# Two interleaved transformer layers on one core: riders' probabilities turned by a DMA, untiled TensorE groups run as column tiles, and a new order of the work

## The chip, the cores and the metric

The kernel runs on one core of a Trainium2 chip. A core has five engines that work side by side and wait for each other by semaphores: PE (TensorE; its weight loads are the row PEld), DVE (VectorE), ACT (ScalarE), POOL (GpSimd) and SP (SyncE, which issues the transfers here). The metric is the device time of one execution in microseconds, as the median of several runs; lower is better.

## The reference

Four sub-layers follow one another over 2048 tokens of width 448, each added to its input: attention with a recurrent memory (A), a gated MLP (B), A again, B again, with the same weights both times.

```python
def A(x, mem0, Wq, Wk, Wv, Wo):        # 64 segments of 32 tokens, 16 heads of 256
    mem = mem0                          # 8 rows
    for s in range(64):
        h = concat([mem, x[32*s:32*s+32]])             # 40 rows
        q, k, v = h @ Wq, h @ Wk, h @ Wv               # per head
        p = softmax(mask(q @ k.T / 16))                # 40 x 40; a token sees the memory rows and earlier tokens
        o = sum over heads of (p @ v) @ Wo
        mem, out[s] = o[:8], o[8:]
def B(x): return (relu(x @ W_gate) * (x @ W_up)) @ W_down      # 448 -> 1792 -> 448
x = x + A(layernorm(x)); x = x + B(layernorm(x)); x = x + A(layernorm(x)); x = x + B(layernorm(x))
```

## The kernel before

**Folding.** At the start `weights` forms one product of Wq and Wk for every head (tile `A`, SBUF) and one of Wv and Wo (`Bsb`). For that each weight half of 256 columns is turned on PE against an identity (`transposes`, L709, eight 128-column turns), copied to SBUF, and multiplied (`product`, L722). The raw Wq and Wk come by DMA into eight staging slots `Wst`; a head pair `g` takes four slots, and each slot is one load of 512 columns in two transfers (`load`, L684). The first product needs the turned first halves of all four slots. A warm-up group `spin` (L627) of 11 matmuls on zeros stands at the head of the program's list.

**The chain.** Segment s needs the memory that segment s-1 leaves. `chain(step)` runs steps 0 to 70: the memory rows of layer 0 at segment `step` and of layer 1 at segment `step - 7` go together. One step is: memory times `A` (L891, 64x32 tiles), copy and turn on DVE (L1065, L1073), scores (`middle`, L1088), softmax on DVE and ACT, turn P on PE (L1121) and copy it (`PT`), P times h (L1145, L1148), times `Bsb` (L932, 128x32 column tiles, 56 matmuls), split into two bf16 parts (`Ohi`, `Olo`), back into rows of the next memory (`cols`, L951, eight matmuls of 32 columns). The new rows `Rsb` go to the tiles `HR` by a copy for layer 0 and by small DMAs for layer 1.

**Riders.** L891 and L932 have room for 32 rows, and the memory uses 16. From step 7 on the other rows carry token rows of layer 1's even tiles, the "riders" (66 passes of `middle` with a mask, of lower rank than the chain; their y is needed by the next step's L932). Their rows leave by small DMAs `Tsb<-Rsb`.

**Tiles.** The token rows proper are worked per 128 tokens: `att_group` (L1234 in 64x128 tiles, scores L1260, softmax, turn of P L1279, y L1145, output L1309 untiled in three groups of 5, 5 and 4 matmuls of 448 columns), the MLP (`glu_units` L1333 in 64x128 tiles, `glu_down` L1352 untiled), and `norm` with a turn on PE (L1180).

**Order.** `_Sched` lists every operation with engines, a cost in ns, what it reads and writes, and a `mode`: 0 untiled, 1 column tiles of 128x32, 2 row tiles of 64x128, 3 column halves, 4 tiles of 64x32. The order of PE is written out by hand: each character of the string `LINE` says which of the groups still left comes next (a `~` skips 80). The other engines' orders come out of the planner `schedule`, by earliest start, rank and `ORDER`, with fixed costs: 94 ns (`TURN`) where PE's mode changes, 2400 ns (`LAND`) from a transfer to its landing. A gap that it foresees on PE is filled with dummy matmuls (`filler`, L1367). Every engine then runs its list strictly in order. DMAs take semaphores in turn out of `N_DMA` = 48; at the end SP waits for the last 48 (L392 to L395).

Of the kernel before, what the change touches and what calls it, by code (L numbers as in the profile page):

```python
# [32 lines left out]
ORDER = ("apBEFEsrpdlvwtalsfVTmkVGVHZcgovZUZYfyHHZvnNZAeQbcMbewfTnUFUQvUgaoeqBAiOnO0I0rv0lMkrKnz0r0uAaQNEaNQQazYeabwswaa"  # L33
         "kachNaueDaDnraBi0VaaaEgchNAXKfqPTdYLCyXA0vXuAOMMuO0NTaaajla0sKIRXEYQtW000wNsLjwIkZxNdPhpEaFWfCWPsaP0azdGgppTTs"
         "bfxQ0LhUZmVLLYpzOWWVheCpFacuzUaZoawVWvTdGTClViASRXlmhReM0pS0nuALXNRpGATz0RgjtdlAlInioyUoUnX0EJmWLBaQraHHgEouJy"
         "bgxcnwtPWaEwhaPDlTbAvF0FJZnHqUttyQIg0otagAaIklTzbYuw0squomrJAAAsAxgfYHR0c0f0YCdJKysxYHj0zmAgzyluvSEk0aKpSp0AIl"
         "SAhJiaASaAjxutpkdukQvXH0pf0d0OUdICCoteize0GWGJgbDCAYcYyuaUPaFwGEN0ufHAAosgdnlSiXvsBKRpLSPeJ0U0AdQQNoVdiAxBtbcm"
         "hQfFe0gK0z0El0XzAABafzaoEaRbnwtcelFvOzxSIHsgGuHAIXeDJAP0AXYdLdduBBRaXAXlTaR0a0BUMhhWLAelHAaP0DgayjFfYkBiBuWidV"
         "WiEYJkPoVscRkU0GPwDmebCeAxOwj0KcwGOspsFauwazTgIY0HfAEv0KtqKAaSmMagVKYxtbPQOj0vhW0wZWXdckUYaxYatAjeUTDVfArZgA0J"
         "ZxLSOaznuQoCnfqdyEgiNX0bmeNghhUWctiX0XITkAZNUhGAcyoSAUWPa0AakgETBEqGbfApnOAwd0yYs0eQWssMwOfAn0lAmfLvjLZA0WHaMq"  # L40
         "abHJwwdZxSpjVJqGdIaXVYVftvYDmJPTLpTmjnssZgsANROGVOcAKzpflogjfAdoanAANOKUraGtaGmvpaa0iLDhoZulYn0fTqA0TAG00EKzbs"
         "wtVAqHgyXueoaSNaspOSrpZ0RHCRikLlDqA0KoMwXoONJmAPmqdyWy0ijMNrHoTONMl0YhHFxhyjwdAtY0o0gTyWaDQdadZNmT0zs0gVmtaaaa"
         "aag0fNKUTaaaaaaaaaaaaaaaaaaaqjtECNTsaxWawbsV")

SIGNS = "ABCDEFGHIJKLMNOPQRSTUVWXYZabcdefghijklmnopqrstuvwxyz0123456789+-*/=<>()[]{}.,:;!"
LINE = ("IGGFNNMLGGFHFFOFMBJIHHFFEFEMMLFHFEEFEMEBLAAEEFDDBBBBIIDDDDCCBBBIIFBBBDBBABAIHEEBACBAJBLAOHLFBDCCAAgAeeAdBFBCLA"
        "XoBAEUCTBBSBQBKOCBMECBABHUAGGBAAbBAQBJAQAWAFBADPAECCCADIMFIIALEOOEFLEGAEDGFACAABAAWAAAKARBAPHdAcGASAQAAABT~EA~"
        "DAihKA(DAdAAbAa9AZZZAAXBAAADTSDDAAAAMAAKKKJAIIAHAHGABBDAABBAAAAAATMYYAAWKcKKZAM~JNAVkLA~MAAAEEAHDAaZFFCCGCASBB"
        "QABOSAAMMMAAKALLuA0KICIHHLHHHAGGGGGAAADJAABBAEAAAABAMAAXXQAGIaASHHWAGAAAFQDBDDAFBEEYXAAFAASAAQCBOARNNNAALANM4A"
        "uLJQCJIIBHHHAFGFnHGFcAADAABBAEAAABCAAMBAXXQAJcKJZSALeAdLKAAAQEEIATDA87GneF3CC7A0BEyAfDDuuuAAsAEtsFEoAACmCAkSoh"  # L50
        "hhKggg9BAeIVfeABAAaYEAAAVATTLAAQQQDAAONGOAONBfAVcLUACHAHMGGaBFFFBUAGDRKDxxF~PETAtGACqAAoNDClllmAAJQDAgfACB=ccc"
        "ADACCAWAbAUATAWSSSA0zDQARQAAOAAALAJJCIIIALIHAUIIgAeAGAAaEABQKBBaJIiBBBUFHBEBPAD}{DtsCA>BB=[CA*OCB999ALAC55mD44"
        "Ck1AAzADAwABWycsjBBpppApf=nDFnmlDDPDhDAlfCCdDcccCebAabbaBGBFIAUAAAAWQIDOUDNNNAPAAvDIIAH87CNCV3AAA05CzIyyyCHxAA"
        "uuBKssAQQwpJDAAlC(BjAJhhhDAAeC/BeeADAZDCAXAAAUAYTStSSSASgBCAAAMAAYABBbVIAAneTGGQZgAFXAAbPDAB5B3MLBBBFFJFBADA>>"
        "FRQE[*mABB8B7ACA8HBB111AEAyAAxxmdvAAbiqqvIpFFFmmmFdlFjFFjiAA/GD+leAAHbiaaBHYYYCJCWVAqVVUAC0dARAAAOBS0NCBAKKKNK"
        "JDKI54DVHDAAyADAv0DuMCsssABDpAHnoo.CMCAADiAnCffGCdAcccEAAaZACBXXAAAATpwTYAtRAQAPPPBAAMAAZAAkAJHaUfVHHHjAAPFAQA"
        "kUMDAABLeBBBaHBEB}{NHACC>CQCA*GA+jAA777AA65BA65AbAi1zADYAwAvuktttAtAaADoFppDDnDDTiNDDgGfLydDcccFcAacAcbBFBWXAG"
        "AaATASRXEDPPPAANPAM=/DAJA9<ZIA6A5NM3334AkLAYAPxDvAvuCTCAEAoAOAlGpCj.Biii-EAgAfCCeeAEAAAgZ2CBXAWVAAASSSASgABAAN"
        "AAAYACAjVIZBATSHGZgGARAADjASCBWLLcBBBLFPFBEAA)(FQFCHC-CC9AJB-A5nB333BkcFziAzzFYEAvA0AUsqhqp{pppBBAmmRAllRACOAA"
        "fAAjAcAbaAZZZAbYJXGYXIBUAGSAAAPUAOFNNNFNAVVvLEASI87hDID+3AAF0ADyYxxxAxAvAAuuALAJqACHtNAlBj>jBADgggEDAAcEAcc8ED"  # L60
        "AAWeXAAAUZASSkSSSAnSBABAAALAAWAiAHTYAAcRFFhPfFAAcPMDARAJJBIaILBBBJtUIFBEBPHDDA88ppEECC28lHCABxBAv~KvvvXDtAAUss"
        "ADEpAumEmlCk<kkkCaNhABhhEKDcAcIRZZAAcXBWWWFNBUTGBSSSFAEgOVOAAAAKDQOEITDLHHHIAAFKAAABxwBLBKbrEBBuHnAmNBkkkLBjiA"
        "DIggE.DdAAEaAAYAX*CBVVVAVATAAUTRAoQQDBOBNAMMMdALLAZAADCAHTYAnGGQQZZEFRdSRFAZSED3DDDHHDGDI]]ItISLFDA*AC+Ak8AA+6"
        "667AA4CG43BFAAzAAxB1vveuuudAAurrjutqAFADoxuEDkl+DkjGiiiDiMDDgeeDEfeDbbDDZKeDDWdDNU9DTTTATARKADZZOvQDdWAMATLBRL"
        "QQQEQAANJNPPDGCJAKAAGACFAEDXDDDATCABBPWIHAAZAQAWJOAIICQDDAAGDDAEDABEAIEDAAAAAADBAAADAAAACAAAAAA")


class _Op:
    __slots__ = ("idx", "engs", "cost", "fn", "deps", "prio", "dma", "eng", "ndep", "users", "ready",
                 "start", "end", "need_inc", "val", "clock", "slot", "seq", "alloc", "mode",  # L70
                 "touch", "busy", "cross", "at")
# [16 lines left out]
class _Sched:  # L88
# [5 lines left out]
    N_DMA = 48  # L94
# [28 lines left out]
    def add(self, engs, cost, fn, r=(), w=(), prio=None, dma=0, alloc=(), room=(), mode=0, now=None, busy=None, cross=False, at=0):  # L123
# [7 lines left out]
        o.at = at  # L131
        o.deps = {}
# [62 lines left out]

    def schedule(self):
# [35 lines left out]
        while left:  # L232
# [55 lines left out]
            if o.dma:  # L288
                free[e] = t0 + c
                dma_free = max(dma_free, t0) + o.dma / 240.0  # L290
                o.end = dma_free + self.LAND
# [32 lines left out]
    def filler(self, n, ns, bank, deps, start, seq):  # L324

        f = _Op()
        f.at = 0
        f.idx, f.engs, f.cost, f.eng, f.dma, f.touch, f.mode = -1, ("pe",), {"pe": n * ns}, "pe", 0, [], 0
# [11 lines left out]
    def emit(self, nc, stack, block):  # L340
# [41 lines left out]
        def run(eng, E):  # L382
            if eng == "act":
                E.preload_act_table_set("natural_log_exp_and_others")
            for o, waits, inc in plans[eng]:
                for key, v in waits:
                    E.wait_ge(dsem[key[1]] if isinstance(key, tuple) else sems[key], v)
                ins = o.fn(E, eng)
# [30 lines left out]
def copy_any(out, in_, scale=None):  # L419
# [8 lines left out]
    return fn  # L428

# [54 lines left out]
class _Kernel:  # L484
# [39 lines left out]
    def alloc(self):  # L524
# [32 lines left out]
        for p in range(NPAIR):  # L557
            for k in range(4):
                for hh in range(2):
                    c = D * (b_idx(k, p, hh) if k < 3 else b_tail(p))  # L560
                    self.s.alias[("B", p, hh, k)] = [(w, i) for w in ("Wst", "Wst3", "Wst4") for i in range(12) if c < 2048 * i + 2048 and 2048 * i < c + D]
# [45 lines left out]
    def constants(self):  # L607
# [17 lines left out]
        def spin(E, e):  # L625
            for _ in range(11):
                i = E.matmul(wb.ap()[:, 0:D], lhsT=hG[:, 0:128], rhs=hG[:, 128:576], start=True, stop=True)  # L627
            return i
        s.add("pe", 11 * 378, spin, r=hk, w=[wb], alloc=[wb])
# [45 lines left out]
    def dma(self, dst, src, nbytes, r=(), w=(), prio=None):  # L675
        return self.s.add("sp", 750 if nbytes < 8192 else 640, lambda E, e: E.dma_start(dst, src), r=r, w=w, dma=nbytes, prio=prio)

    def turned(self, dst, src, nbytes, r, w, prio=None):

        self.s.add("sp", 900, lambda E, e: E.dma_start(dst, src, transpose=True), r=r, w=w, dma=4 * nbytes, prio=prio)  # L680

    def weights(self):
        s = self.s
        def load(src, p, slot):  # L684
            s.part()
            c0 = 512 * p
            self.dma(self.Wst[slot][:, 0:3, :], src[64:448, c0:c0 + 512].rearrange("(k p) c -> p k c", p=128), 393216,
                     w=[("Wst", slot)])
            if slot < 8:
                self.dma(self.Wst[slot][0:64, 3, :], src[0:64, c0:c0 + 512], 65536, w=[("Wst3", slot)])  # L690
            else:
                self.dma(self.Wst[slot][0:64, 3, 0:256], src[0:64, c0:c0 + 256], 32768, w=[("Wst3", slot)])
                self.dma(self.Wst[slot][64:128, 3, 256:512], src[0:64, c0 + 256:c0 + 512], 32768, w=[("Wst4", slot)])

        def transposes(slot, hh, wt, rot):
# [4 lines left out]
            keys = [("Wst", slot), ("Wst3", slot), ("Wz", slot, 0)] + ([("Wst4", slot), ("Wz", slot, 1)] if slot >= 8 else [])  # L700
# [161 lines left out]
    def chain(self, step):  # L862
# [84 lines left out]
        def cols(E, e):  # L947
            for k in range(4):
                for q, O in enumerate((hi_, lo_)):
                    w = O[:, 128 * ((k + 1) % 4):128 * ((k + 1) % 4) + 128]  # L950
                    x = E.matmul(br.ap()[:, 32 * k:32 * k + 32], lhsT=w, rhs=self.Sel[:, :], start=(q == 0), stop=(q == 1))  # L951
            return x
        s.add("pe", mm_cost(*[32] * 8), cols, r=["Ohi", "Oli", "Oh2", "Ol2", "Sel"], w=[br], alloc=[br], room=MEM + ["mC"], **P)
# [26 lines left out]
        for slot, q, o in out:  # L980
            for v in range(4):
                to, of = self.row_piece(self.Tsb[32 * q + 8 * o:32 * q + 8 * o + 8, :], R[32 * v + 8 * slot:32 * v + 8 * slot + 8, :], v)
                self.dma(to, of, 2048, r=[rk], w=[("Tsb", q, o, v)])
# [91 lines left out]
    def middle(self, act, m, row, col, P):  # L1075
# [32 lines left out]
        else:  # L1108
# [7 lines left out]
            for c, sg, l in act:  # L1116
# [3 lines left out]
        bp = self.bank("C", "G")  # L1120
        s.add("pe", 56, lambda E, e: E.matmul(bp.ap().bitcast(BF)[:, 0:128], lhsT=m["P"][:, :], rhs=self.ident[:, :], is_transpose=True),  # L1121
              r=[k_("P"), k_("P0"), k_("P1"), "ident"], w=[bp], alloc=[bp], **P)
        s.add(EV, ev_cost(128, fast=True), copy_any(m["PT"][0:104, :], lambda: bp.ap().bitcast(BF)[0:104, 0:128]), r=[bp], w=[k_("PT")], **P)
# [33 lines left out]
    def norm(self, t, dst):  # L1157
# [20 lines left out]
        def tr(E, e):  # L1178
            for k, o in enumerate(BLOCK):
                x = E.matmul(pk()[:, k, :], lhsT=xn[:, o:o + 128], rhs=self.ident[:, :], is_transpose=True)  # L1180
# [311 lines left out]
```

## Time and profile before

| | |
|---|---|
| time, median of 3 runs | 1509.2 us (1508.84 to 1509.79) |
| the profiled execution | 1510.83 us, of which the span from first to last instruction is 1509.0 us |
| PE busy | 1486.1 us (98%), 36999 matmuls |
| DVE, ACT, POOL busy | 77%, 59%, 8% |
| bytes moved by DMA | 34 MB, nearly all in the first 65 us |
| share of PE in the chain that ended last | 95% |

A line of a group gives line, engine, operation, output<-inputs, shapes, count, then busy time in us and mean ns of one, then the engine's idle time before them and what ended it. Matmuls are pipelined, so one of 448 columns shows as 353 ns while the next starts 189 ns later; what counts for PE's time is the distance from start to start. A timeline line gives start in us, length in us, and what ran.

### The profile page before, as it was taken

What the parts mean: (1) busy time and instruction counts of PE and PEld (TensorE: products, weight loads), DVE (VectorE), ACT (ScalarE), POOL (GpSimd) and SP (SyncE); (2) the same over time, 40 slices, a digit from 0 to 9 for tenths busy, and PEclk for the clock granted to TensorE, in tenths of its full rate; (3) what the DMA queues carried; (4) which work ended last, traced back from release to release, by engine and by line L of the source; (5) the groups of instructions that cost most, each with busy time, mean ns of one, the idle gap of its engine ahead of it and who ended that gap; (6) DMA issues with size and microseconds to landing.
All of it is one profiled execution on the core that took longest, in us unless ns stands there. A gap on an engine that the chain in (4) does not pass through costs nothing.

```text
span 1509.0 us, 82702 instructions
## 1 busy us (share of the span) xinstructions
PE 1486.1 (98%) x36999; PEld 1059.0 (70%) x36999; DVE 1167.8 (77%) x3574; ACT 891.9 (59%) x2407; POOL 120.1 (8%) x483
## 2 busy tenths in 40 slices
PE   7999999999999999999999999999999999999999
PEld 5657666666767777777767677777768777677776
DVE  6767788788888888687877788788877788688764
ACT  8775465566555656565655556566555556555543
POOL 1000000010000010000000010010100000010000
PEclk9999999999999999999999999999999999999999
DMA  8512100000000000000000000000000000000000
GB/s 244 169 30 74 40 8 12 11 9 8 8 5 12 11 8 15 4 18 4 18 5 8 14 9 14 4 18 6 17 6 8 14 8 15 5 8 8 11 6 14
DMA packets 60658, 34.08 MB, mean 23 GB/s; under 512 B 31744, under 2 KB 60176, under 8 KB 60304
## 3 DMA queue, kind: packets, MB, share of 16 engines
q1 hardware_dynamic: 60304, 28.80, 7.4%
q8 instruction: 291, 4.77, 1.3%
q14 instruction: 63, 0.52, 0.1%
HBM read 21.36 MB, written 1.84 MB: 15 GB/s over the span
## 4 chain that ended last, share of the span: by engine, by line
PE 95%; DVE 2%; ACT 1%; DMA 1%; issue 1%; SPq 0%; POOL 0%; DVEq 0%
PE psG L1234 17%; PE psG L1309 17%; PE psG L1333 11%; PE psC L932 10%; PE psC L891 8%; PE psG L1352 5%; PE psG L891 4%; PE psG L1145 3%; PE psG L722 3%; PE psG L1260 3%; PE psC L1088 2%; PE psC L1145 2%; PE psG L709 1%; PE psG L932 1%; PE psG L1180 1%; PE psC L951 1%
## 5 line engine op out<-in xcount | busy, mean ns | idle before, releaser
L1234 PE MATMUL psG<-HT,A 64*128 64x128 bf16 x4924 | 287.2, 216 | 1.0 <-issue 0.6
L1309 PE MATMUL psG<-Bsb,YT 128*128 128x448 bf16 x1344 | 286.2, 353 | 0.0
L1234 PE MATMUL psG<-HX,A 64*128 64x128 bf16 x3693 | 267.6, 216 | 0.0
L1234 PEld LDWEIGHTS psG<-HT,A 64*128 64x128 bf16 x4924 | 235.7, 94 | 14.0 <-issue 8.3
L424 ACT ACTIVATE Ug<-psG 64x128 bf16<-64x128 f32 (+2 forms) x456 | 160.7, 372 | 63.7 <-PE psG L1234 54.7
L1234 PEld LDWEIGHTS psG<-HX,A 64*128 64x128 bf16 x3693 | 195.2, 94 | 0.1
L1309 PEld LDWEIGHTS psG<-Bsb,YT 128*128 128x128 bf16 x1344 | 118.1, 97 | 97.9 <-issue 7.8
L1333 PE MATMUL psG<-G,glu 64*128 64x128 bf16 x5880 | 185.6, 216 | 0.7 <-issue 0.4
L1333 PEld LDWEIGHTS psG<-G,glu 64*128 64x128 bf16 x5880 | 171.8, 94 | 11.2 <-issue 8.4
L932 PE MATMUL psC<-Bsb,YTm 128*32 128x448 bf16 x3304 | 167.3, 353 | 0.3
L1065 DVE STREAM_TRANSPOSE uT<-Usb 128x384 bf16<-128x384 bf16 x280 | 154.6, 559 | 6.1 <-ACT Usb L424 1.8
L891 PE MATMUL psG<-A,mT 64*32 64x448 bf16 x4004 | 144.8, 350 | 0.5 <-issue 0.5
L891 PE MATMUL psC<-A,mT 64*32 64x448 bf16 x3836 | 140.8, 350 | 0.1
L424 ACT ACTIVATE YT<-psG 128x448 bf16<-128x448 f32 x254 | 128.3, 544 | 10.3 <-PE psG L1148 8.9
L932 PEld LDWEIGHTS psC<-Bsb,YTm 128*32 128x32 bf16 x3304 | 82.8, 97 | 65.1 <-ACT YTm L424 1.6
L427 DVE CAST Ug<-psG 64x128 bf16<-64x128 f32 (+2 forms) x250 | 104.8, 430 | 16.0 <-PE psG L1234 11.8
L940 ACT ACTIVATE Ohi<-psC 128x448 bf16<-128x448 f32 x122 | 46.9, 384 | 116.4 <-PE psC L932 85.5
L1338 ACT ACTIVATE hG<-psG 128x512 bf16<-128x512 f32 (+1 forms) x125 | 67.7, 543 | 72.3 <-PE psG L1333 65.6
L891 PEld LDWEIGHTS psC<-A,mT 64*32 64x32 bf16 x3836 | 71.9, 92 | 50.0 <-DVE mT L427 3.9
L941 DVE TENSOR_TENSOR Olo<-psC,Ohi 128x448 bf16<-128x448 f32 x122 | 51.4, 422 | 71.5 <-ACT Ohi L940 70.8
L1339 DVE TENSOR_TENSOR hG<-hG,psG 128x512 bf16<-128x512 bf16 (+1 forms) x116 | 70.7, 614 | 29.5 <-ACT hG L1338 28.0
L1352 PE MATMUL psG<-glu,hG 128*128 128x448 bf16 x420 | 92.4, 352 | 0.0
(223 smaller groups left out, 2874.4 us busy)
## 6 DMA issues: line engine op xcount, KB each, us to landing
HR<-xn SPq DMA_DIRECT2D x128, 32.0 KB
Tsb<-Rsb SPq DMA_DIRECT2D x256, 1.5 KB
Tsb<-Rsb SPq DMA_DIRECT2D x256, 2.0 KB
Bsb<-in_A_Wq_dram SPq DMA_DIRECT2D x8, 384.0 KB
Bsb<-in_A_Wk_dram SPq DMA_DIRECT2D x8, 384.0 KB
HR<-Rsb SPq DMA_DIRECT2D x126, 1.5 KB
HR<-Rsb SPq DMA_DIRECT2D x126, 2.0 KB
X<-in_A_x_dram SPq DMA_DIRECT2D x16, 112.0 KB
```

The costliest lines, as they stand in the source:

```text
L424: return E.activation(out, i, ACT.Copy, scale=1.0 if scale is None else scale)
L427: return E.tensor_copy(out, i)
L891: i = E.matmul(ub[v].ap()[32 * j:32 * j + 32, 0:D], lhsT=self.mT[rw, WHERE[b], first:first + 32], rhs=cols, start=(b == 0), stop=(b == 6), ...
L932: x = E.matmul(bo.ap()[32 * j:32 * j + 32, 0:D], lhsT=self.YTm[:, q, :], rhs=self.Bsb[:, chunks[q], :], start=(i == 0), stop=(i == 13), ti ...
L1065: self.s.add("dve", 578, lambda E, e, out=out, hh=hh: E.transpose(out, heads[hh]), r=[("Usb", 2 * half + v) for v in range(2)], w=[f"uT{ha ...
L1145: return E.matmul(ps[:, n * q:n * q + n], lhsT=HR[rows, 128 * q:128 * q + 128], rhs=PT, start=True, stop=True, tile_position=(b, 0))
L1234: i = E.matmul(ub[v].ap()[:, 128 * n:128 * n + 128], lhsT=self.A[rw, b, a0:a0 + 128], rhs=HT[rw, WHOLE[b], :, 0:SEG] if CROSS[b] is None e ...
L1309: i = E.matmul(bo.ap()[:, 0:D], lhsT=YT[:, c, :], rhs=self.Bsb[:, 14 * g + c, :], start=(g == 0 and c == 0), stop=(g == 3 and c == 13))
L1333: i_ = E.matmul(two[v].ap()[:, 128 * c:128 * c + 128], lhsT=self.Wgu[rw, b, f0:f0 + 128], rhs=G[rw, WHOLE[b] if CROSS[b] is None else 4 + ...
L1338: s.add("act", 170 + 0.833 * N, lambda E, e, dst=dst, z=two[0], N=N: E.activation(dst, z.ap()[:, 0:N], ACT.Relu), r=[two[0]], w=[("hG", i, ...
L1339: s.add("dve", dv_cost(N), lambda E, e, z=two[1], N=N, dst=dst: E.tensor_tensor(dst, dst, z.ap()[:, 0:N], ALU.mult), r=[two[1]], w=[("hG", ...
L1352: i_ = E.matmul(bk.ap()[:, 0:D], lhsT=hG[:, c, :], rhs=self.Wd[:, c, :], start=(c == 0), stop=(c == NFC - 1))
```

## The change

- **Riders' P.** In `middle`, where there is a mask, the turn on PE and the copy from PSUM are left out; `turned` issues a transposing DMA on SP from P to PT. Planned cost: 1400 ns on SP, 3500 ns to land.
- **Column tiles.** A group may name a second mode: `also=(1,)`. `line` goes through the order, keeps runs of groups whose modes agree, and gives each run one mode, the lowest possible. So an untiled group becomes mode 1 only where it stands in a run with a group that is mode 1 alone (L932, and the two first steps' L999 and L1022). In mode 1 `packed` issues four matmuls of 32 output rows in place of one of 128. The groups that may do so: L1309, L1352, L1279, L1180, L951, and L1121 (the chain's).
- **First weights in halves.** The four loads of the first head pair are split into columns 0 to 255 and 256 to 511, first halves first, with the highest rank. The warm-up has 17 matmuls.
- **The plan.** 96 semaphores for DMAs in place of 48; 3500 ns to land for `HR<-xn`, `Tsb<-Rsb` and the turned P; new strings `ORDER` and `LINE`. (The name of the change speaks of blocks of 256 instructions: no line of the diff has them; they can only have gone into the strings.)

```diff
-    N_DMA = 48
+    N_DMA = 96
...
-        return out + left
+        out += left
+        run, have = [], None
+        for o in out + [None]:
+            may = {o.mode, *o.also} if o else set()
+            if have is not None and not have & may:
+                for x in run:
+                    x.mode = min(have)
+                run, have = [], None
+            have = may if have is None else have & may
+            run.append(o)
+        return out
...
+def packed(E, mode, out, lhsT, rhs, **k):
+
+    if mode != 1:
+        return E.matmul(out, lhsT=lhsT, rhs=rhs, **k)
+    for j in range(4):
+        q = slice(32 * j, 32 * j + 32)
+        i = E.matmul(out[q], lhsT=lhsT[:, q], rhs=rhs, tile_position=(0, 32 * j), **k)
+    return i
...
-            for _ in range(11):
+            for _ in range(17):
...
-        self.s.add("sp", 900, lambda E, e: E.dma_start(dst, src, transpose=True), r=r, w=w, dma=4 * nbytes, prio=prio)
+        self.s.add("sp", 1400, lambda E, e: E.dma_start(dst, src, transpose=True), r=r, w=w, dma=4 * nbytes, prio=prio, land=3500.0)
...
-                    load(W, g + 4 * v, slot[v, i])
+                    load(W, g + 4 * v, slot[v, i], (0, 1) if g else (0,))
+            if not g:
+                for v in range(2):
+                    for i, W in enumerate((self.Wq_d, self.Wk_d)):
+                        load(W, g + 4 * v, slot[v, i], (1,))
...
-                    x = E.matmul(br.ap()[:, 32 * k:32 * k + 32], lhsT=w, rhs=self.Sel[:, :], start=(q == 0), stop=(q == 1))
+                    x = packed(E, e, br.ap()[:, 32 * k:32 * k + 32], w, self.Sel[:, :], start=(q == 0), stop=(q == 1))
...
+        if m["mask"] is not None:
+            self.turned(m["PT"][:, :], m["P"][:, :], 32768, [k_("P"), k_("P0"), k_("P1")], [k_("PT")], prio=P["prio"])
+            bp = None
+        else:
+            bp = self.bank("C", "G")
...
-                    i = E.matmul(bo.ap()[:, 0:D], lhsT=YT[:, c, :], rhs=self.Bsb[:, 14 * g + c, :], start=(g == 0 and c == 0), stop=(g == 3 and c == 13))
+                    i = packed(E, e, bo.ap()[:, 0:D], YT[:, c, :], self.Bsb[:, 14 * g + c, :], start=(g == 0 and c == 0), stop=(g == 3 and c == 13))
```

More of the change, by code (lines that the diff above doesn't have):

```diff
@@ L121, in part, with add @@
         self.shift = 0.25 * (STEPS.index(ORDER[self.unit]) - 26) if self.unit < len(ORDER) else 0.0
-    def add(self, engs, cost, fn, r=(), w=(), prio=None, dma=0, alloc=(), room=(), mode=0, now=None, busy=None, cross=False, at=0):
+    def add(self, engs, cost, fn, r=(), w=(), prio=None, dma=0, alloc=(), room=(), mode=0, now=None, busy=None, cross=False, at=0, also=(), land=None):
         o = _Op()
@@ L131, in add @@
         o.at = at
+        o.also = also
+        o.land = land or self.LAND
         o.deps = {}
@@ L290, in schedule @@
                 dma_free = max(dma_free, t0) + o.dma / 240.0
-                o.end = dma_free + self.LAND
+                o.end = dma_free + o.land
             elif e == "pe":
@@ L678, in turned, with load @@
     def turned(self, dst, src, nbytes, r, w, prio=None):
-        self.s.add("sp", 900, lambda E, e: E.dma_start(dst, src, transpose=True), r=r, w=w, dma=4 * nbytes, prio=prio)
+        self.s.add("sp", 1400, lambda E, e: E.dma_start(dst, src, transpose=True), r=r, w=w, dma=4 * nbytes, prio=prio, land=3500.0)
     def weights(self):
         s = self.s
-        def load(src, p, slot):
-            s.part()
+        def load(src, p, slot, halves=(0, 1)):
+            if halves != (1,):
+                s.part()
@@ L686, in load @@
             c0 = 512 * p
+            if slot < 8:
+                a, b = 256 * halves[0], 256 * halves[-1] + 256
+                n = b - a
+                self.dma(self.Wst[slot][:, 0:3, a:b], src[64:448, c0 + a:c0 + b].rearrange("(k p) c -> p k c", p=128), 768 * n,
+                         w=[("Wst", slot, h) for h in halves], prio=0 if len(halves) == 1 else None)
+                self.dma(self.Wst[slot][0:64, 3, a:b], src[0:64, c0 + a:c0 + b], 128 * n, w=[("Wst3", slot, h) for h in halves],
+                         prio=0 if len(halves) == 1 else None)
+                return
@@ L982, in chain @@
                 to, of = self.row_piece(self.Tsb[32 * q + 8 * o:32 * q + 8 * o + 8, :], R[32 * v + 8 * slot:32 * v + 8 * slot + 8, :], v)
-                self.dma(to, of, 2048, r=[rk], w=[("Tsb", q, o, v)])
+                self.dma(to, of, 2048, r=[rk], w=[("Tsb", q, o, v)], land=3500.0)
         for f in late:
@@ L1119, in middle @@
                       r=[k_("Em"), k_("rc")], w=[k_(f"P{c}")], **P)
[L1120 to L1123, printed above, removed]
+        if m["mask"] is not None:
[3 more added lines that the diff above has]
+            bp = self.bank("C", "G")
+        if bp: s.add("pe", 56, lambda E, e: packed(E, e, bp.ap().bitcast(BF)[:, 0:128], m["P"][:, :], self.ident[:, :], is_transpose=True),
+              r=[k_("P"), k_("P0"), k_("P1"), "ident"], w=[bp], alloc=[bp], also=(1,), **P)
+        if bp: s.add(EV, ev_cost(128, fast=True), copy_any(m["PT"][0:104, :], lambda: bp.ap().bitcast(BF)[0:104, 0:128]), r=[bp], w=[k_("PT")], **P)
         yb = [self.bank("C", "G") for _ in act]
@@ L1179, in tr @@
             for k, o in enumerate(BLOCK):
-                x = E.matmul(pk()[:, k, :], lhsT=xn[:, o:o + 128], rhs=self.ident[:, :], is_transpose=True)
+                x = packed(E, e, pk()[:, k, :], xn[:, o:o + 128], self.ident[:, :], is_transpose=True)
             return x
@@ L1187, in norm @@
             G = self.G2[g]
-            s.add("pe", mm_cost(*[128] * 4), tr, r=xnk + ["ident"], w=[bk], alloc=[bk], room=[("G2", g, v) for v in range(3)])
+            s.add("pe", mm_cost(*[128] * 4), tr, also=(1,), r=xnk + ["ident"], w=[bk], alloc=[bk], room=[("G2", g, v) for v in range(3)])
             s.add(EV, ev_cost(512, fast=True), copy_any(G[:, 0:4, :], pk), r=[bk], w=[("G2", g, 0)])
@@ L1195, in norm @@
         HT, HX = self.HT[l][b], self.HX[l][b]
-        s.add("pe", mm_cost(*[128] * 4), tr, r=xnk + ["ident"], w=[bk], alloc=[bk], room=[("HTx", l, b), ("HX", l, b, 0), ("HX", l, b, 1)])
+        s.add("pe", mm_cost(*[128] * 4), tr, also=(1,), r=xnk + ["ident"], w=[bk], alloc=[bk], room=[("HTx", l, b), ("HX", l, b, 0), ("HX", l, b, 1)])
         for p in range(2):
@@ L1278, in pt @@
             for p in range(2):
-                i = E.matmul(bp.ap().bitcast(BF)[:, 128 * p:128 * p + 128], lhsT=Pf[:, 128 * p:128 * p + 128], rhs=self.ident[:, :],
-                             is_transpose=True)
+                i = packed(E, e, bp.ap().bitcast(BF)[:, 128 * p:128 * p + 128], Pf[:, 128 * p:128 * p + 128], self.ident[:, :], is_transpose=True)
             return i
-        s.add("pe", mm_cost(128, 128), pt, r=[("Px", si), "ident"], w=[bp], alloc=[bp], room=["PTx"])
+        s.add("pe", mm_cost(128, 128), pt, r=[("Px", si), "ident"], w=[bp], alloc=[bp], room=["PTx"], also=(1,))
         s.add(EV, ev_cost(256, fast=True), copy_any(PT[0:104, :], lambda: bp.ap().bitcast(BF)[0:104, 0:256]), r=[bp], w=["PTx"])
@@ L1351, in fn @@
                 for c in range(4 * q, 4 * q + n):
-                    i_ = E.matmul(bk.ap()[:, 0:D], lhsT=hG[:, c, :], rhs=self.Wd[:, c, :], start=(c == 0), stop=(c == NFC - 1))
+                    i_ = packed(E, e, bk.ap()[:, 0:D], hG[:, c, :], self.Wd[:, c, :], start=(c == 0), stop=(c == NFC - 1))
                 return i_
-            s.add("pe", mm_cost(*[D] * n), fn, r=[("hG", i, q), f"Wd_{q}"], w=[bk], alloc=[bk] if q == 0 else ())
+            s.add("pe", mm_cost(*[D] * n), fn, r=[("hG", i, q), f"Wd_{q}"], w=[bk], alloc=[bk] if q == 0 else (), also=(1,))
         self.add_x(t, bk)
```

91 lines of the change are left out of this document (45 added, 46 removed).

## The prediction, made before the changed kernel ran

> **What bounds the kernel now.** I read first the shares of the chain that ended last and the slices of the page, then the groups by line, then PE's timeline.
>
> ```profile
> PE   7999999999999999999999999999999999999999
> ...
> PE 95%; DVE 2%; ACT 1%; DMA 1%; issue 1%; SPq 0%; POOL 0%; DVEq 0%
> ...
> L1309 PE MATMUL psG<-Bsb,YT 128*128 128x448 bf16 x1344 | 286.2, 353 | 0.0
> L932 PE MATMUL psC<-Bsb,YTm 128*32 128x448 bf16 x3304 | 167.3, 353 | 0.3
> ```
>
> PE is the bound from 8.6 us on, so only what PE's own sequence loses or gains counts; ACT and DVE work that disappears is worth nothing. I therefore split the span by PE's records, start to start: nothing until 8.6 us; 1417 us in which groups stream (among them 5.4 us of filler matmuls and 6.5 us of pauses inside groups); some 615 changes of tile shape; 17.4 us of pauses over 20 ns at 81 group borders beyond the cost of a change; 3 us of tail. Walking `LINE` over the list of groups gives 614 changes of mode, so string and trace agree. The price of one change is seen here:
>
> ```profile
> 708.28 0.93 PE L1352 MATMUL psG<-glu,hG 128*128 128x448 bf16 x4
> ...
> 709.45 0.22 PE L1121 MATMUL psC<-ident,Pr 128*128 128x128 bf16 x1
> 709.51 0.92 PE L1352 MATMUL psG<-glu,hG 128*128 128x448 bf16 x4
> ...
> 710.26 0.18 PE L951 MATMUL psC<-Sel,Ohi 128*128 128x32 bf16 x1
> 710.29 0.18 PE L951 MATMUL psC<-Sel,Olo 128*128 128x32 bf16 x1
> ...
> 714.18 0.35 PE L891 MATMUL psG<-A,mT 64*32 64x448 bf16 x1
> 714.47 0.34 PE L1145 MATMUL psG<-PTx,HR 40*128 40x128 bf16 x6
> ```
>
> From the last start of L891 (714.18) to L1145 (714.47) are 290 ns; 448 columns stream in 190, so the change costs about 95. Over all records the median is 92 to 98 ns for every pair of shapes. One rider's turn is 54 to 60 ns of PE (709.45 to 709.51). L951 places matmuls of 32 columns 25 ns apart.
>
> **1. Changes of mode.** Walking the new `LINE` with the rule of `line` gives 579 changes, 35 fewer: 35 x 95 = **-3.3 us**. Without the second mode the same order would have 660. The runs turn 80 groups of L1309, 16 of L1352, 26 of L1279, 20 of L1180 and 24 of L951 into column tiles; the chain's L1121 never.
>
> **2. The riders' turns.** 66 x 54 ns = **-3.6 us**. Leaving them out alone changes no count of modes (36 of 66 stand between untiled groups).
>
> **3. The price of column tiles.** For 448 columns there is a row: 56 matmuls of L932 take 2667 ns, 14 of L1309 take 2640, so 27 ns in 14, some 9 ns for a group of 5: 96 x 8 = +0.7 us. For 128 and 32 moving columns in four tiles no row exists. Lower end: the tiles run side by side, and a group only pays some 12 ns of stagger (the four starts of L932 lie 3 to 4 ns apart): 70 x 12 = +0.9. Upper end: each small load and matmul takes the 25 ns of L951, one after another: L1279 8 x 25 = 200 in place of 109, L1180 16 x 25 = 400 for 221, L951 32 x 25 = 800 for 192; 26 x 91 + 20 x 179 + 24 x 608 = +20.5 us. Nearest is L891: eight loads and matmuls start within 27 ns and repeat every 191 ns, 23.9 ns each, set by the 448 columns and not by loads; and L1148 (two row tiles of 64 columns) starts one every 14 ns. Both speak for side by side: **+1.6 us**.
>
> The Trainium skill (TensorEngine Tiling, Restrictions and Gotchas) says that column tiling excludes the fast weight load; its page TensorE: Matmul & The Clock Gate (LDWEIGHTS) prices a load at columns / 1.2 ns, so an estimate of 27 ns for 32 columns, as much as a full fast one. If four such loads queue, that is the upper end above; L999, four tiles of 256 columns, repeats every 0.11 us, which neither shows nor excludes it.
>
> **4. The head.**
>
> ```profile
> 8.57 1.89 PE L709 MATMUL psG<-ident,Bsb 128*128 128x128 bf16 x16 [8.57 <-DMA Bsb<-in_A_Wk_dram]
> ...
> 11.32 3.29 PE L709 MATMUL psG<-ident,Bsb 128*128 128x128 bf16 x40
> 14.54 2.84 PE L722 MATMUL psG<-glu 128*64 128x448 bf16 x28
> ...
> 21.87 2.41 PE L709 MATMUL psG<-ident,Bsb 128*128 128x128 bf16 x40
> ...
> 28.36 2.24 PE L627 MATMUL psC<-hG 128*128 128x448 bf16 x11
> ...
> 30.55 2.84 PE L722 MATMUL psG<-glu 128*64 128x448 bf16 x28
> ```
>
> The first 16 turns stand 110 ns apart, those at 21.87 about 56: PE starts at half speed and speeds up near 13 us. The first product comes at 14.54, after seven groups of turns. Now the 17 warm-up matmuls run from about 1.3 us while PE would idle, so the turns run at 56 ns. A transfer takes 0.58 us of SP; its first packet comes 1.1 us after its issue, its semaphore 1.3 us after the last. The new order turns the four first halves, then the second halves of slots 0 and 2, before the first product. Slot 2's second half is the 13th and 14th transfer, issued to 8.9 us, landed near 11.4 us; 0.45 us for its turns: first product at 11.9, with six groups done instead of seven: 14.54 - 11.9 - 0.45 = **-2.2 us** (0 if packets of 512 bytes or the copies behind the turns hold it up; -4.5 if the data comes as early as it is wanted). SP's later loads are moved back by 8 more issues, 4.6 us; the first product of the second pair is wanted after 18 us, when they have landed. The 11 warm-up matmuls at 28.36 disappear: the products behind them have their inputs by about 29 us, so 30.55 - 28.95 = **-1.6 us** (0 to -2.1).
>
> **5. Fetches of instructions.** Counting PE's instructions, some 14 pauses with no wait fall on position 193 to 195 of a block of 256, in all 4.0 us. The diff has nothing for them but the order itself; the column tiles add some 4400 instructions to 74000. **-2 us** (-4 to +1).
>
> **6. Other stalls and fillers.** 17.4 + 6.5 + 5.4 us of pauses and fillers, less the fetches and the filler in the head (1.0), leave some 24 us. Here the planner's belief matters: it gave a transfer 2.4 us to land.
>
> ```profile
> 846.26 3.45 DMA HR<-xn
> ...
> 850.45 3.68 DMA Tsb<-Rsb
> ...
> 855.97 0.37 PE psC L951 x8
> ```
>
> DVE waits in order for `Tsb`, the chain's `Olo` behind it is late, and PE stands 1.15 us before L951. The new 3.5 us is right for these. Only a few stalls have such a cause; most lie at 100 to 350 us, where the chain has too little other work. The new order's distances in the chain (L951 to L891, L1088 to L1121) are equal or a little longer. **-3 us** (-10 to +5).
>
> **7. The turned P as a wait.** P to PT took 0.53 us on PE and ACT; now SP needs 1.4 us by the plan, and PE waits in order at the rider's L1145, with the whole kernel behind it. The score's start to P took 3.5 us in the median. Between a rider's scores and its y the new order puts at least 6.9 us of PE work; 4 riders have under 8, 12 under 9, 17 under 10. A transposing DMA has no row. Lower end: 3.45 us, as `HR<-xn` of the same 32 KB; upper: 16384 single elements at 8 ns (the smallest packets) on 16 engines add 8.2, so 11.6 us. I take 4.5 as it is nearest to the row of equal size: ready 8 us after the scores, and the shortfall below 8 us sums to 3.2, of which the quickest P save a part: **+2 us**. On SP 66 x 1.4 = 92 us join 697; behind one stand only transfers for the next step, some ten us away.
>
> The Trainium skill (Advanced Engine Details and Errata, X-Bar Transpose) holds transposing transfers to be as fast as plain ones; by it this term would be about 0; no run here shows it yet.
>
> **8. The tail.** After the last store SP waits for 48 semaphores in pairs, 61 ns each, from 1507.08 to 1508.56; the store had landed by then. 48 more are 24 x 61 = **+1.5 us**.
>
> **Sum.** -3.3 - 3.6 + 1.6 - 2.2 - 1.6 - 2 - 3 + 2 + 1.5 = -10.6. The profiled execution took 1510.83, so 1500.2; the median lies 1.6 below that execution: **1498.6 us**.
>
> **Rivals.**
> - *The stalls stay* (0.16): the new order is no better in places 4 (first term), 5 and 6, and only what is counted remains: -10.6 + 7.2 = -3.4, 1505.8. For it: the order before came from the same planner and still left 24 us.
> - *The column tiles' loads queue* (0.08): term 3 becomes 0.7 + 20.5, so +9.0, 1518.2, slower. It decides from half of the upper end on. Against it: L891 and L1148.
> - *The turned P lands late* (0.13): slower. Place: L1145 of the riders; if PT is ready 10 us after the scores instead of 8, the shortfalls of 17 riders sum to 23.8 us: -10.6 - 2 + 23.8 = +11.2, 1520.4. At 9.2 us it eats the whole gain; at 15 us it would be 150 us.
> - *The forecast* (0.63).
>
> Faster or slower by under 0.2% (3 us) is about what a measurement cannot tell from no change. Faster: 0.63, most of the first rival, and mild forms of the others, 0.76; same 0.08; slower 0.16. The range takes the good ends of 4 to 6 (some -10) and reaches to mild forms of the two slower rivals: 1488 to 1514.
>
> **What would show it.** Changes of tile shape near 579; L709 at 56 ns from the first; first L722 near 12 us; no L627 later; no PE wait for a DMA at L1145 of PTr; a packed L951 group of some 0.2 us (0.8 if loads queue), from its first start to the next group; SP's last waits 3 us long. I am wrong if PE waits for PTr in dozens of places, or if fillers and pauses add up to more than the 29 us of before.

## The result, and the profile after

The changed kernel takes **1514.69 us** (median of 6 runs, 1512.50 to 1516.30) where the kernel before takes 1509.61 beside it: ratio **1.0033 (95%: 1.0020 to 1.0046)**, some 5 us slower. 1498.6 was predicted, in a range up to 1514. The profiled execution has a span of 1513.3 us, 4.3 more than before.

From the page of the changed kernel: PE's slices, the shares of the chain that ended last, and the group that was L932 before.

```profile
PE   8999999999999999999999999999999999999998
...
PE 94%; DVE 3%; ACT 2%; issue 1%; POOL 0%; DVEq 0%; POOLq 0%
...
L966 PE MATMUL psC<-Bsb,YTm 128*32 128x448 bf16 x3472 | 178.1, 353 | 0.9 <-DVE YTm L440 0.8
```

PE is still the bound, and its first slice is fuller (the warm-up runs from 1.2 us), but DVE and ACT have won two points of the chain: PE stands behind them more often. To see where, I set the traces side by side at the same finished work of PE (every group at one standard price; riders' turns, fillers and warm-up matmuls count as none). Microseconds behind the kernel before, when that kernel stood at the time on top:

| | 13.6 | 27.4 | 35.2 | 45.3 | 61.6 | 100.6 | 875.9 | 1493 |
|---|---|---|---|---|---|---|---|---|
| changed | -0.2 | +0.8 | -1.2 | +0.3 | **+4.1** | +4.2 | +1.9 | +3.6 |

After 62 us the changed kernel gains little and gives it back; single executions of the same instructions drift 1 to 2 us apart there, so the last two columns say no more than that. The loss sits between 35 and 62 us. First the stretch where it was to win, PE of the changed kernel:

```profile
1.22 6.13 PE L651 MATMUL psC<-hG 128*128 128x448 bf16 x17 [1.22 <-DVE hG L646]
7.29 1.96 PE L739 MATMUL psG<-ident,Bsb 128*128 128x128 bf16 x32
11.95 0.62 PE L739 MATMUL psG<-ident,Bsb 128*128 128x128 bf16 x8 [2.71 <-ACT glu L437]
12.41 1.17 PE L1404 MATMUL psC<-ident 128*128 128x128 bf16 x18
13.41 0.61 PE L739 MATMUL psG<-ident,Bsb 128*128 128x128 bf16 x8
13.95 2.84 PE L752 MATMUL psG<-glu 128*64 128x448 bf16 x28
```

The turns are warm (32 in 1.96 us), yet the first product starts at 13.95, not 11.9: PE waits 2.71 us for an ACT copy. ACT in the same stretch:

```profile
7.61 3.49 ACT L437 ACTIVATE glu<-hG 64x256 bf16<-64x256 bf16 x8
11.00 2.52 ACT L437 ACTIVATE glu<-psG 128x896 bf16<-128x896 bf16 x3
```

Until 11.0 us ACT copies zeros (`glu<-hG`, fills of the staging slots); only then come the turned weights (`glu<-psG`) that were in PSUM from 9.25 us on. Now the stretch of the loss, PE of the changed kernel and of the kernel before:

```profile
47.99 1.07 PE L739 MATMUL psG<-ident,Bsb 128*128 128x128 bf16 x16
48.89 0.61 PE L1404 MATMUL psC<-ident 128*128 128x128 bf16 x8
49.77 0.55 PE L752 MATMUL psG<-glu 128*128 128x448 bf16 x2 [0.27 <-DVE glu L440]
50.16 1.06 PE L739 MATMUL psG<-ident,Bsb 128*128 128x128 bf16 x16
...
56.24 0.55 PE L1404 MATMUL psG<-A 128*128 128x448 bf16 x2
57.03 1.52 PE L925 MATMUL psC<-A,mT 64*32 64x448 bf16 x56 [0.24 <-DVE A L439]
```

```profile
47.33 2.41 PE L709 MATMUL psG<-ident,Bsb 128*128 128x128 bf16 x40
49.58 3.69 PE L722 MATMUL psG<-glu 128*128 128x448 bf16 x32
```

Before, forty turns (five groups) are followed by 32 product matmuls without a gap: the copies of the first turns end while PE turns the last. After, two groups of turns are followed at once by the product that needs their copies; fillers (L1404) and waits stand where the copies run. In the stretch that holds this loss (34.0 to 65.7 us of the changed kernel) fillers take 3.6 us and waits 1.8, where the same work of the kernel before has no filler and under 0.2 us of waits. Some 2 us stand at the three places of this kind (43.8, 48.9 and 51.4 us), 0.8 at 56.2, where the first product with `A` stands right behind the copy into `A`, 0.5 at 61.4 is a late fetch of instructions (last section), and most of the rest waits for ACT's copies of earlier products.

### The profile page after: what moved, and what is told of

Same layout as the page of the kernel before. It is cut to its first block, busy times and chain, and to the rows that moved or that the text cites. A ratio compares the mean times of both kernels' runs of the same rounds, so it can differ in the third digit from the quotient of the medians.

```text
span 1513.3 us, 87244 instructions
## 1 busy us (share of the span) xinstructions
PE 1489.1 (98%) x39223; PEld 1066.7 (70%) x39223; DVE 1166.3 (77%) x3552; ACT 884.8 (58%) x2365; POOL 117.6 (8%) x481
## 4 chain that ended last, share of the span: by engine, by line
PE 94%; DVE 3%; ACT 2%; issue 1%; POOL 0%; DVEq 0%; POOLq 0%
PE psG L1272 17%; PE psG L447 17%; PE psG L1370 11%; PE psC L966 11%; PE psC L925 9%; PE psG L450 5%; PE psG L925 4%; PE psC L447 3%; PE psG L1183 3%; PE psG L752 3%; PE psG L1298 3%; PE psC L1183 2%; PE psC L1122 1%; PE psG L966 1%; PE psG L739 1%; PE psG L1186 1%
## 5 line engine op out<-in xcount | busy, mean ns | idle before, releaser
L447 PE MATMUL psG<-Bsb,YT 128*128 128x448 bf16 x875 | 186.7, 352 | 0.0
L966 PE MATMUL psC<-Bsb,YTm 128*32 128x448 bf16 x3472 | 178.1, 353 | 0.9 <-DVE YTm L440 0.8
L925 PE MATMUL psG<-A,mT 64*32 64x448 bf16 x4116 | 159.7, 350 | 1.0 <-issue 1.0
L925 PE MATMUL psC<-A,mT 64*32 64x448 bf16 x3724 | 150.6, 350 | 1.2 <-DVE mT L440 0.4
L437 ACT ACTIVATE YT<-psG 128x448 bf16<-128x448 f32 x245 | 124.0, 544 | 20.2 <-PE psG L1186 19.4
L966 PEld LDWEIGHTS psC<-Bsb,YTm 128*32 128x32 bf16 x3472 | 88.1, 97 | 67.0 <-DVE YTm L440 2.5
L447 PEld LDWEIGHTS psG<-Bsb,YT 128*128 128x128 bf16 x875 | 76.2, 97 | 58.6 <-issue 1.1
L975 DVE TENSOR_TENSOR Olo<-psC,Ohi 128x448 bf16<-128x448 f32 (+1 forms) x128 | 54.1, 422 | 79.0 <-ACT Ohi L974 78.5
L974 ACT ACTIVATE Ohi<-psC 128x448 bf16<-128x448 f32 (+1 forms) x128 | 49.1, 384 | 104.6 <-PE psC L966 72.1
L925 PEld LDWEIGHTS psG<-A,mT 64*32 64x32 bf16 x4116 | 84.1, 92 | 21.1 <-issue 2.5
```

Source lines behind the costliest of these rows:

```text
L437: return E.activation(out, i, ACT.Copy, scale=1.0 if scale is None else scale)
L447: return E.matmul(out, lhsT=lhsT, rhs=rhs, **k)
L925: i = E.matmul(ub[v].ap()[32 * j:32 * j + 32, 0:D], lhsT=self.mT[rw, WHERE[b], first:first + 32], rhs=cols, start=(b == 0), stop=(b == 6), ...
L966: x = E.matmul(bo.ap()[32 * j:32 * j + 32, 0:D], lhsT=self.YTm[:, q, :], rhs=self.Bsb[:, chunks[q], :], start=(i == 0), stop=(i == 13), ti ...
```

## The experiments

All ratios are against the kernel before, run on the same chip at the same time; 0.001 is 1.5 us. "Behind" means the table above.

### e1 to e3: the head's order and the halves, apart

Theory A: the halves make SP the limit, later loads land late, PE runs dry. Theory B: the new order of the first 66 us is itself poor. e1 takes the old order of PE's first 120 groups (and the old `ORDER` of the weights) and whole loads; e2 only whole loads; e3 only the old order. In e1 and e3 two lines keep the old limit of open loads in this stretch; e1 has the old warm-up, e3 the 17 matmuls first. Edit of e1 beside the strings:

```diff
-                    load(W, g + 4 * v, slot[v, i], (0, 1) if g else (0,))
-            if not g:
...
+                    load(W, g + 4 * v, slot[v, i])
+            if 48 <= n < 112:
+                o.deps[self.dmas[n - 48]] = True
-            for _ in range(17):
+            for _ in range(11):
```

> The changed kernel, but its first 120 groups of PE (up to about 64 us) stand in the order of the kernel before, with the whole first loads, the 11 warm-up matmuls at their old place, the old order of the loads and at most 48 of them open at a time in this stretch. The rest is the changed kernel. Both theories (A: the halves make SP the limit, the later loads land some 2 us later and PE runs dry at 44 to 66 us; B: the new order of the first 66 us itself puts products straight behind the copies that they need) give back the 4.1 us by which the changed kernel lies behind at 66 us: 1514.7 - 4.1 = 1510.6, PE's pauses in the first 100 us near 5 us in place of 14.8. If the loss sits in the body, it stays at 1514 to 1515.

> The changed kernel with one edit: the first four slots are loaded whole (8 transfers in place of 16); the new order and the 17 warm-up matmuls stay. Theory A (late loads): the loads land as early as before (3.9 MB by 16 us in place of 3.0), the pauses at 44 to 66 us go, 1510.5 to 1512. Theory B (the order itself): the pauses at 44 to 66 us stay, and the head is no better or worse because the order is made for halves, 1514 to 1518.

> The other corner: the first 120 groups in the order of the kernel before, but the first four slots in halves and the 17 warm-up matmuls first. Theory A: the loads are as late as in the changed kernel and PE loses as much, 1514 to 1517, the pauses sitting where products wait for turned weights that wait for loads. Theory B: the pauses at 44 to 66 us go, 1510 to 1512.

| | whole loads | halves |
|---|---|---|
| old order of the head | e1: 1.0011 (1.0003 to 1.0020) | e3: 1.0055 (1.0041 to 1.0068) |
| new order of the head | e2: 1.0047 (1.0033 to 1.0061) | the change: 1.0033 |

Behind at 35.2 and 61.6 us: e1 -0.7 and -0.7; e2 +0.8 and +5.7; e3 +3.9 and +7.5; the change -1.2 and +4.1. So e1 gives the head back, as both theories wanted. e2 speaks for B and against A: its loads are ahead of the kernel before (7.9 MB landed by 30 us, against 7.2 before and 6.8 in the change), and it loses the same 5 us with the same gaps:

```profile
50.86 0.61 PE L1400 MATMUL psC<-ident 128*128 128x128 bf16 x8
51.75 0.55 PE L752 MATMUL psG<-glu 128*128 128x448 bf16 x2 [0.27 <-DVE glu L440]
```

In the change, too, the data is there: by the semaphores that the turns wait for, the weights turned between 42 and 66 us had landed 5 to 17 us earlier (those of the 16 turns at 47.99 us between 39.5 and 41.3). That the turns stand too close to their products is read from these traces alone: no run moves only them apart. e3, however, shows that A is no fiction for the *old* order: with halves it stands 5.1 us in one filler ahead of turns that wait for loads.

```profile
18.94 5.13 PE L1406 MATMUL psC<-ident 128*128 128x128 bf16 x89
```

Transfers of half the size move less in the same issues. The rows of 5 to 10 us, before and after (last column GB/s; e2 with whole loads in the new order has 283, e3 with halves in the old one 192):

```profile
5.00:10.00 5.00, 1.43 (x14) 1.43 (x15) 1.12 (x6) 4.73 (x12) 2.26 (x11) 1.00 0.98 287
```

```profile
5.00:10.00 5.00, 4.25 (x40) 2.59 (x38) 2.37 (x8) 4.73 (x12) 2.26 (x11) 1.00 0.67 189
```

The halves and the new order thus belong together: from e1 to e3 the old order loses 6.6 us (the place of the warm-up, which also differs, is worth under 1 us between e8 and e11 below); the new order is no slower with halves than without (1.0033 against 1.0047), and pays 5 us of its own. Whether every order that fits the halves must pay so was not tried.

### e4 and e5: the column tiles

e4 is the change without the second mode, e5 the kernel before with it (order, loads, 48 semaphores and landing times as before; P turned on PE).

```diff
-            may = {o.mode, *o.also} if o else set()
+            may = {o.mode} if o else set()
```

> The changed kernel without the second mode: every group stays untiled as in the kernel before, order and all else as changed. 660 changes of tile shape in place of 579: 81 x 95 ns = +7.7 us, less the 2.3 us that the column tiles themselves cost by the trace: +5.4, 1520.1. If the column tiles cost more than the trace shows (their extra instructions fetched late), less: 1517 to 1519.

> The kernel before, order and all, with the second mode alone: 586 changes of tile shape in place of 614, 28 x 95 ns = -2.7 us; 134 groups as column tiles at the prices of the changed kernel's trace (some 15 ns each in the mean) = +1.9. If that is all: 1509.6 - 0.8 = 1508.8. If the column tiles also bring later fetches of instructions in many executions, 1510 to 1512 with a wider spread.

e4: **1.0049** (1.0036 to 1.0063), 2.4 us slower than the change where 5.4 was expected, at the lower edge of the 1517 to 1519 for dearer tiles. e5: **1.0005** (0.9995 to 1.0015), no difference. The counts of changes are as expected (660, 586). In the traces 81 more changes cost e4 7.6 us, and small differences at other borders 1.8; it saves 3.2 of the tiles' own price and 1.0 of waits ahead of `cols` (8.5 against 9.5 us in the body): 5.2, as expected. But its execution also has 2.3 us less of instruction fetches, mostly chance (below), and the two traces differ by 1.6 us only, so another 1.3 us is not accounted for. The medians give 2.4 us, give or take some 2.8; 5.4 lies just beyond, so what the second mode is worth stays open between nothing and some 5 us. The tiles themselves run side by side. Changed kernel, `cols`:

```profile
857.75 0.20 PE L450 MATMUL psC<-Sel,Ohi 128*32 128x32 bf16 x4 [0.39 <-DVE Olo L975]
857.79 0.19 PE L450 MATMUL psC<-Sel,Olo 128*32 128x32 bf16 x4
857.82 0.19 PE L450 MATMUL psC<-Sel,Ohi 128*32 128x32 bf16 x4
```

Four tiles start together every 25 to 30 ns, as one untiled matmul did: 213 ns for the group in place of 192.

### e6: the turned P without the new order

Order, loads and warm-up of the kernel before, the column tiles as in e5, but P turned by DMA. The plan is told 1.11 us of SP and a landing 1.9 us after the issue. (In the change's trace that is when the last data packet ends where nothing else is under way; the semaphore, which PE waits for, is complete 2.2 us after the issue at the earliest and 2.4 in the median, so the plan was some 0.5 us too hopeful.) Of the edit, the line of the plan:

```diff
-        self.s.add("sp", 1400, ..., prio=prio, land=3500.0)
+        self.s.add("sp", 1110, ..., prio=prio, land=1350.0)
```

> The order, the whole first loads and the 11 warm-up matmuls of the kernel before, with the riders' P turned by DMA, the column tiles, 96 semaphores and the plan told of the measured time of a turning transfer (1.1 us of SP, landed 1.9 us after its issue). Theory C (the turned P costs nothing even in the old order, so the new order was not needed for it): a rider's P is ready 3.5 us after its scores, 5.6 with the transfer; in the old order's trace one rider has less than that, so -3.5 for the turns, -0.8 for the tiles, +1.5 for the tail: 1506.8. Theory D (the order is what makes it cheap: SP is taken by the rows that the chain sends when a P comes, and one PTr buffer holds a second rider back): PE waits for PTr at half a dozen places or more of 1 to 5 us, 1512 to 1525.

**1.0192** (1.0177 to 1.0208), 29 us slower: theory D, and beyond its range. PE waits at nine riders' y, 23 us in all with the fillers put there (0.1 us in the change). SP and PE at the dearest of them:

```profile
842.99 2.90 SPq L702 DMA_DIRECT2D HR<-Rsb  x4
845.93 5.78 SPq L702 DMA_DIRECT2D Tsb<-Rsb  x8
851.76 3.70 SPq L702 DMA_DIRECT2D HR<-xn  x4
855.50 1.24 SPq L706 DMA_TRANSPOSE PTr<-Pr  x1
```

```profile
851.46 3.94 PE L1402 MATMUL psG<-A 128*128 128x448 bf16 x20
857.91 0.23 PE L1181 MATMUL psC<-PTr,HR 40*128 40x128 bf16 x1 [2.51 <-DMA PTr<-Pr]
```

P was ready at 849.9 (DVE's last write of `Pr`), but seven of these sixteen transfers still stood ahead of it on SP, 0.72 us each for `Tsb` and 0.93 for `HR<-xn`, which makes 5.6 us. The transfer itself is quicker: issued at 855.50, used at 857.91. What costs is the queue. In the change half of the 66 P are issued within 0.03 us of being ready, and the five that wait over 2 us on SP (at most 6.2) have their y late enough: none of the riders' y comes less than 4.1 us after its P.

### e7 and e12: the tail

The change (e7) and the kernel before (e12), where SP waits at the end only for transfers that no instruction waited for (four stores).

```diff
-                    if o.dma:
+                    if o.dma and not o.users:
```

> The changed kernel, but after its last transfer SP waits only for those of the last 96 transfers that no instruction has waited for (4 stores to the output). 92 waits fewer, 46 pairs at 61 ns = -2.8 us: 1511.9. If the waits lie beside other work (the last store's landing), less, down to 0.

> The kernel before with the short tail alone: some 44 of its last 48 waits go, 22 pairs at 61 ns = -1.3 us, ratio 0.9991. If so, e8's lead over the kernel before is the tail and nothing else.

e7: 1.0021 (1.0009 to 1.0033); from PE's last start to the end 3.2 us in place of 4.8: 1.6 us, where 2.8 was expected, or less. e12: 1.0002 (0.9994 to 1.0011), 3.2 in place of 3.3: nothing, where 1.3 us was expected. In the kernel before the waits lay beside the landing of the last store; of 96 only the second half sticks out.

### e9, e10 and e14: ACT's fills of zeros

e9 puts the 16 fills for slots 8 to 15 on POOL. e10 changes one term of the plan: it tells it what they cost. e14 puts them behind the copies in the kernel before (with e12's tail). The edit of e10:

```diff
-                    s.add("act", ev_cost(cols.stop - cols.start)["act"], copy_any(to, of), r=hk, w=[("Wz", i, n)])
+                    s.add("act", (630 if i < 8 else 545) + (1500 if i == 4 else 0), copy_any(to, of), r=hk, w=[("Wz", i, n)])
```

> The changed kernel, but the 16 fills of zeros for slots 8 to 15, which ACT copies one every 0.44 us (the last ends at 11.09 us, and the first three copies of turned weights stand behind them on ACT), are memsets on POOL. If these copies are what holds the first product at 13.95 us: it comes near 12 us, and 2 us of it stay to the end: 1512.7. If the weights' own landing holds it, the first product stays at 13.5 to 14 and the time at 1514 to 1515; if later loads take the gain back, the first product is early and the time still 1514.

> The changed kernel, with the plan told what these fills cost on ACT (0.44 us apart in place of 0.28, the first ending 1.5 us later): it then puts ACT's copies of turned weights ahead of the last fills; PE's and SP's order stay. The copies then start near 9 us in place of 11.0: the same as e9 within 0.5 us, 1512.7 to 1513.2, by the first theory; 1514.7 by the others.

> The kernel before with the short tail (e12, ratio 1.0002), and the fills of slots 8 to 15 put behind ACT's copies of turned weights. If the fills hold its first product (14.54 us) too and nothing hides it: first product near 13 us, -1.5 us, ratio 0.9992. If the 11 warm-up matmuls at 28 us and the loads behind them hide it: first product earlier, the group after the warm-up matmuls at the same time as before, ratio 1.000.

e9: **1.0017** (1.0008 to 1.0026); e10: **1.0015** (1.0006 to 1.0024); 2.4 and 2.7 us of the change's 5 are gone (each give or take some 2). ACT and PE in e10:

```profile
7.61 1.29 ACT L437 ACTIVATE glu<-hG 64x256 bf16<-64x256 bf16 x3
8.92 0.92 ACT L437 ACTIVATE glu<-psG 128x896 bf16<-128x896 bf16 x1
```

```profile
10.73 0.61 PE L739 MATMUL psG<-ident,Bsb 128*128 128x128 bf16 x8 [0.23 <-DMA Bsb<-in_A_Wq_dram]
11.27 2.84 PE L752 MATMUL psG<-glu 128*64 128x448 bf16 x28
```

One copy goes ahead of the last fills, the first product starts at 11.27 (11.43 in e9), and now the last wait before it is for the data. Behind at 13.6 and 61.6 us: e10 -2.8 and +1.9, the change -0.2 and +4.1: the gain stays. The 5 us between 35 and 62 us are lost all the same. e14: 1.0003 (0.9993 to 1.0012), first product 13.95 after turns that begin at 11.50: in the old order with whole loads the product comes 0.6 us earlier without the fills ahead of it, and nothing of that stays.

### e8, e11 and e13: the best of both

The old head with whole loads, the new body and the short tail: e8 with the 17 warm-up matmuls first, e11 and e13 with 11 at the old place (and the fills' cost as in e10), e13 with the fills behind the copies. The old head is 140 groups long here.

> As e1 (old order of the head, here the first 140 groups, whole first loads), with the 17 warm-up matmuls first in place of 11 at 28 us, and the short tail of e7. From e1's 1511.0: -2.8 for the tail, -1.6 for the warm-up matmuls at 28 us that are gone, 0 to -0.7 for warm first turns: 1506, faster than both kernels. If the products at 28 us wait for their data anyway, 1508.

> As e1 (old order of the head, here 140 groups, whole first loads, 11 warm-up matmuls at 28 us) with the short tail of e7 and the costs of the fills as in e10. From e1's ratio of 1.0011: the short tail saves 1.8 us, the fills nothing here (the plan of this head does not change before 9 us): 1509.3, against the kernel before within 0.1%. The warm-up matmuls first (e8) were then worth nothing either if this is as fast as e8.

> As e11 (old order of the first 140 groups, whole first loads, 11 warm-up matmuls at 28 us, short tail), with the fills of slots 8 to 15 put behind ACT's copies of turned weights. If the old head gains from it, the first product comes 1 to 2 us earlier and the time is e11's ratio of 0.9997 less 0.001: 0.9987. If the head is bound by its loads from 28 us on, the first product is early and the time is e11's.

e8: 0.9991 (0.9982 to 1.0000); e11: 0.9997 (0.9988 to 1.0005); e13: 1.0003 (0.9994 to 1.0012). All are faster than the change, and none is clearly faster than the kernel before. Warm-up first and late fills bring nothing here: in this head PE waits for its loads near 10 and 30 us anyway. The whole new body, with its 6.8 us of counted savings, is worth nothing measurable: dearer tiles, pauses and fetches (below) eat them.

## Why the prediction was wrong

Eight steps summed to -10.6; the two profiled executions differ by +4.3.

- **Steps 1 and 2** held: 579 changes, -3.3 us (not counting those that fillers add; with them the traces have 615 and 588); the riders' turns are gone, -3.5.
- **Step 3**, +1.6, is +2.5 by the groups' own times (L951 192 to 213 ns, L1309 of four 754 to 775), and another 1.0 of waits ahead of `cols`. Its rival, queueing loads, is dead: L951's group would have taken 800 ns. The Trainium skill (TensorEngine Tiling, Restrictions and Gotchas) would have let one expect it, since column tiling there excludes the fast weight load; this trace shows no more than the 21 ns of a group for it.
- **Step 4, first term**, -2.2, **failed**: "Slot 2's second half is the 13th and 14th transfer ... first product at 11.9" followed only the data, which landed at 10.7 and 10.85. ACT's fills held the copies until 11.0, the product began at 13.95, and the change won 0.2. e9 and e10 show the cause, and that the path of the data was right: without the fills ahead the product starts at 11.3 to 11.4. The row was there to be read. In the kernel before, ACT also copies zeros until 11.0 us:

```profile
7.61 3.48 ACT L424 ACTIVATE glu<-hG 64x256 bf16<-64x256 bf16 x8
11.00 0.89 ACT L424 ACTIVATE glu<-psG 128x896 bf16<-128x896 bf16 x1
```

  Naming "the copies behind the turns" as the bad end, without looking at ACT's row, was not enough.
- **Step 4, second term**, -1.6: from +0.8 to -1.2 behind, -2.0. Right, for this order alone; e8 shows that in the old order with whole loads the removed warm-up gains nothing.
- **Step 5**, -2, **failed**: the pauses grow from 4.7 to 6.6 us. Over all traces the kernels with the new body have 3.1 to 7.9 (mean of eleven 5.2), those with the old 3.6 to 4.7 (mean of five 4.2); e9, with the changed kernel's instructions, has 3.9, and e13 7.9 where e11, with the same instructions, has 4.2. So much of it is chance, and the new strings bought nothing.
- **Step 6**, -3, **failed**, and is the largest error: pauses at group borders after 100 us go from 18.8 to 21.5 us (+2.7, of it +2.0 ahead of `cols`), and the head loses 5.3 us between 35 and 62 us. The step credited the new order with fewer stalls on the ground of one stall that it would mend; the 8 us of new ones lie even beyond its bad end of +5. e2 and e1 show that the 5 us come with the order of the head. The 2.7 are not chance either: counted in one way (fillers included) the eleven kernels with the new body have 21.8 to 23.5 us of such pauses, three executions of the old body 19.5 to 20.5. Since e4 without the column tiles has 22.4, it is the order, for the most part; which of its groups, stays open.
- **Step 7**, +2, is -0.4: riders' y waits 0.1 us where it waited 0.6. The wait priced there is real, though, and larger: e6. The step asked who stands *behind* the turned P on SP; the queue *ahead* of it was what could cost 23 us. The transfer lands 2.4 us after its issue in the median, quicker than the lower bound of 3.45 that I took from `HR<-xn`. That bound was a slow row, picked from the chain that ended last: in the same trace the 128 transfers `HR<-xn` land after 1.9 us in the median, and `Tsb<-Rsb` (3.68 in step 6) after 1.8. There the Trainium skill (Advanced Engine Details and Errata, X-Bar Transpose), which holds turning transfers to be as fast as plain ones, was nearer than my 4.5: in the change the plain ones of the same size take 2.2 us, the turned ones 2.4.
- **Step 8**, +1.5, is +1.45 (e7 gives back 1.6), though the reason given is only half right: e12 shows that the first 48 waits are hidden.

Measured terms: -3.3 - 3.5 + 2.5 - 0.2 - 2.0 + 0.9 (between 14 and 27 us) + 5.3 + 1.4 (fetches after 62 us) + 2.7 + 1.5 = +5.3; differences under 20 ns at the borders give -1.3; that makes +4.0 of the +4.3.

## What to carry to other kernels

A new order is an edit of its own: price it stretch by stretch against the order that it replaces (which groups stand between a turn and the product that needs its copy), and do not credit it with stalls mended before counting those that it may add. When a first product is to come earlier, read every engine between the data and it, here ACT with cheap-looking fills that cost 0.44 us each and run strictly in order. For a transfer that something waits for, price the queue ahead of it on the issuing engine (5.6 us in e6) beside its own landing (2.4), and take the landing from the median of all such transfers, not from a row of the critical chain, where the slow ones stand.

## What the runs showed of the hardware that was not expected

- A DMA that turns 128x128 bf16 from SBUF to SBUF takes SP 1.11 us (median) in the change. Counted from the start of the issue, its semaphore is complete after 2.4 us in the median of 66, and after 2.2 at the earliest (plain transfers `HR<-xn` of the same size in the same trace: 2.2 and 1.8). From the view of the tile `PTr` (shortest, median and longest in ns):

```profile
L704 SPq DMA_TRANSPOSE PTr<-Pr x66: 1096/1112/2230, 208.9 to 1445.1; - x66
```

- The next 256 instructions of PE (16 KB, one packet) are fetched when PE passes the border before; from there until they can run 3.2 us pass in the median, 5% over 4.0 (with the 1.4 us from the packet's end to the next instruction that the pauses show). PE pauses where it runs through 256 short instructions faster than that: such pauses stand at one position in the block of 256 and end 1.2 to 1.6 us after the end of such a packet.
- On ACT an SBUF copy of 64x256 bf16 takes 0.44 us from start to start, one of 64x512 0.52 to 0.53: half the columns save less than a fifth of the time.
